# Biased attention with hash-routed experts: 640 slots per expert with an overflow branch, token ids carried in the rows, result rows scattered straight to the output

## The chip, the cores and the metric

The kernel runs on one core of one Trainium2 chip. The metric is device time in microseconds (us) of one execution. Times "of the trace" come from one profiled execution and count from the start of its span.

## The reference

What is computed, cut to what matters (`B=8, H=8, S=576, D=64`; `E=8` experts; `w1` is 512x1024 and `w2` 1024x512 for each expert, both float32):

```python
scores = scale * np.matmul(q, k.transpose(0, 1, 3, 2)) + bias      # bias by |i - j|, per head
attn = exp(scores - max) / sum
x = np.matmul(attn, v)  -> rows of 512 (B*S = 4608 tokens)
expert_idx = token_ids * 2654435761 % 8
for e in range(8):
    mask = expert_idx == e
    out[mask] = np.maximum(x[mask] @ w1[e], 0.0) @ w2[e]
```

With the token ids that are drawn, the experts get 584, 594, 556, 565, 570, 567, 568 and 604 tokens.

## The kernel before, in words

The kernel is written in a tile framework: the program gives loops and tiles, and a scheduler sets the order of each engine's instructions and all waits. An instruction that has nothing to wait for may be put well ahead of its place in the text; on its engine and queue the resulting order is then fixed, and a waiting instruction holds up what is behind it.

**Start.** SP's queue loads constants, the bias table and the token ids (`e2i`, L119: 4608 pieces of 4 bytes), then the first batch's `v` (L218, five loads of pieces of 256 bytes). TensorE and ScalarE make the exponentials of the bias (`ebsb`), which go to DRAM (`t5_ebp`, L111), are spread there to 128 shifted rows per head (`t5_ebr`, `load_ebias`, L195, one copy per head), and come back as one tile `ebias` per head (L203). VectorE meanwhile turns token ids into slots: 8 one-hot masks, prefix sums (L150 to L157) and a row offset from one small matmul; `ds2` holds, for each of 4608 tokens, expert * 768 + rank. One DMA on SP's queue (L357) fills the whole table `t5_xperm` (6144 rows of 512 float16, 6.29 MB) with zeros from a DRAM constant; it stands after batch 0 in the text, and the trace shows where it is issued.

**Attention.** For each of 8 batches, `q` and `k` are loaded on POOL's queue with a conversion from float32 to float16 (L224, L228; two batches of buffers), and for each of four head pairs `m`: transposes (L251), scores (L289), Exp on ScalarE out of PSUM (L297), multiplication by `ebias` on VectorE (L305), the product with `v` (L330), and division into `x_sb` (L348), which holds all tokens. At the end of a batch its 4 or 5 groups of 128 finished rows are scattered into `t5_xperm` by indirect DMAs on POOL's queue (L364). All of these write the same DRAM tensor, so each waits until the one before it has landed. In batch 4 the text has the load and cast of the first expert's `w1` (L373, L377).

**Experts.** For each expert: 768 rows of `t5_xperm` are loaded on SP's queue (`xpn`, L388) and transposed (24 transposes, L399, copied by VectorE, L404). The weights come as float32 on SP's queue (L414, L422; 2.10 MB each) and are cast by ScalarE (`w1`, L419) and VectorE (`w2`, L427). The first layer is 64 matmuls of 384 columns (L434), with a Relu on ScalarE for each four (L440); the second layer is 6 groups of 8 matmuls of 512 columns (L448), each copied by VectorE (`ok`, L455) and stored in slot order into the DRAM tensor `t5_pout` (L457).

**Tail.** When all of `t5_pout` is written, 36 indirect DMAs on POOL's queue gather 128 token rows each (`og`, L460), and SP's queue stores each to the output (L468).

Of the kernel before, what the change touches and what calls it, by code (L numbers as in the profile page):

```python
# [11 lines left out]
F32 = mybir.dt.float32  # L12
F16 = mybir.dt.float16
I32 = mybir.dt.int32
AF = mybir.ActivationFunctionType
# [16 lines left out]
def kernel(  # L32
# [23 lines left out]
    CAP = 768  # L56
    NSLOT = E * CAP
    NPT = DM // P
# [13 lines left out]
    SLT_np = np.triu(np.ones((P, P), dtype=np.float32), 1)  # L72
    Z_np = np.zeros((P, DM), dtype=np.float16)
# [4 lines left out]
    Z_d = nc.inline_tensor(Z_np, "t5_zero")  # L78
# [12 lines left out]
    w1f0 = cst.tile([P, NPT, F], F32, name="w1f0")  # L91
    w1h0 = cst.tile([P, NPT, F], F16, name="w1h0")

    with tc.tile_pool(name="su", bufs=1, side="right") as su, tc.tile_pool(
# [18 lines left out]
        sltsb = su.tile([P, P], F32, name="sltsb")  # L113
        nc.sync.dma_start(out=sltsb[:, :], in_=SLT_d.ap())

        tid32 = moe_token_ids.bitcast(I32)
# [6 lines left out]
        ei = su.tile([P, NGT], I32, name="ei")  # L123
        nc.vector.tensor_scalar(
            out=ei[:, :], in0=e2i[:, :], scalar1=E - 1, scalar2=None,
            op0=ALU.bitwise_and,
        )
        ef = su.tile([P, NGT], F32, name="ef")
        nc.vector.tensor_copy(out=ef[:, :], in_=ei[:, :])

        oh = su.tile([P, E, NGT], F32, name="oh")
        for e in range(E):
# [4 lines left out]
        rowtot = su.tile([P, E], F32, name="rowtot")  # L137
        nc.vector.tensor_reduce(
            out=rowtot[:, :], in_=oh[:, :, :], axis=mybir.AxisListType.X,
            op=ALU.add,  # L140
        )
        partA = sup.tile([P, E], F32, name="partA", space=bass.MemoryType.PSUM)
        nc.tensor.matmul(out=partA[:, :], lhsT=sltsb[:, :], rhs=rowtot[:, :])

        pa = su.tile([P, E, NGT], F32, name="pa")
        pb = su.tile([P, E, NGT], F32, name="pb")
        nc.vector.tensor_copy(out=pa[:, :, :], in_=oh[:, :, :])
        cur, nxt = pa, pb
        sh = 1
        while sh < NGT:  # L150
            nc.vector.tensor_copy(out=nxt[:, :, :sh], in_=cur[:, :, :sh])
            nc.vector.tensor_tensor(
                out=nxt[:, :, sh:], in0=cur[:, :, sh:],
                in1=cur[:, :, : NGT - sh], op=ALU.add,
            )
            cur, nxt = nxt, cur
            sh *= 2  # L157
        exc = nxt
        nc.vector.tensor_tensor(
            out=exc[:, :, :], in0=cur[:, :, :], in1=oh[:, :, :], op=ALU.subtract  # L160
        )
        for e in range(E):
            nc.vector.tensor_scalar(  # L163
                out=exc[:, e, :], in0=exc[:, e, :],
                scalar1=partA[:, e : e + 1], scalar2=None, op0=ALU.add,
            )
        nc.vector.tensor_tensor(
            out=exc[:, :, :], in0=exc[:, :, :], in1=oh[:, :, :], op=ALU.mult
        )
        rank = su.tile([P, NGT], F32, name="rank")  # L170
        nc.vector.tensor_reduce(
            out=rank[:, :], in_=exc[:, :, :].transpose([0, 2, 1]),
            axis=mybir.AxisListType.X, op=ALU.add,
        )
        dsf = su.tile([P, NGT], F32, name="dsf")
        nc.vector.tensor_scalar(
            out=dsf[:, :], in0=ef[:, :], scalar1=float(CAP), scalar2=None,
            op0=ALU.mult,
        )
        nc.vector.tensor_tensor(  # L180
# [318 lines left out]
```

## Time and profile before

| | us |
|---|---|
| median of three timed runs | 706.52 |
| lowest, highest | 705.2, 706.73 |
| span of the profiled execution | 705.6 |
| first multiplication by `ebias` (L305) | 57.4 |
| last division of the attention (L348) ends | 440.2 |
| first transpose of the experts (L399) | 461.5 |
| last matmul of the experts (L448) ends | 643.6 |

| engine | busy us | share of the span |
|---|---|---|
| PE (matmuls) | 556.6 | 79% |
| VectorE (DVE) | 343.5 | 49% |
| ScalarE (ACT) | 290.3 | 41% |
| GpSimd (POOL) | 139.7 | 20% |

How to read it: the span runs from the first to the last instruction of one execution, and the timed median is 0.9 us above it. The four marks of time cut it into a start (to 57), attention (to 440), a hand-over (to 461.5), the experts (to 643.6) and a tail. Shares of the whole span mix these stages, so each stage is read by itself.

### The profile page before, as it was taken

How to read it: one execution, taken by the hardware profiler on the slowest of the kernel's cores; microseconds unless marked ns; L12 is line 12 of the kernel's file. 1: busy time of each engine (PE TensorE's matmuls, PEld its weight loads, DVE VectorE, ACT ScalarE, POOL GpSimd, SP SyncE). 2: the span in 40 equal slices, each digit the busy share in tenths (PEclk: the TensorE clock that was granted, in tenths of full speed). 3: DMA queues.
4: the chain of work that ended last, by engine and by line, in shares of the span. 5: the costliest groups of instructions: out<-in, count | busy, mean ns of one | idle time of the engine just before them, and what ended most of it. 6: DMA issues, size and time to landing. Idle time of an engine off the chain costs nothing.

```text
span 705.6 us, 9655 instructions
## 1 busy us (share of the span) xinstructions
PE 556.6 (79%) x3656; PEld 287.1 (41%) x3656; DVE 343.5 (49%) x1150; ACT 290.3 (41%) x458; POOL 139.7 (20%) x156
## 2 busy tenths in 40 slices
PE   2626999999999999999999998089999999994000
PEld 0202545444444545454444544055555555552000
DVE  3305666666676766667666666024433343312000
ACT  1312365545545453645445463044466545440000
POOL 7213001412323124114110200200000000002772
PEclk9999999999999999999999999999999999998555
DMA  9999980900905819409300000197999997113998
GB/s 111 307 206 262 274 220 24 134 25 18 132 31 33 103 39 67 84 16 86 72 15 1 31 1 1 53 380 278 322 370 334 326 359 265 45 76 127 359 392 283
DMA packets 159614, 110.49 MB, mean 157 GB/s; under 512 B 120520, under 2 KB 131912, under 8 KB 159472
## 3 DMA queue, kind: packets, MB, share of 16 engines
q1 hardware_dynamic: 79952, 86.28, 39.0%
q0 software_dynamic: 79616, 23.60, 26.9%
q8 instruction: 28, 0.46, 0.3%
q14 instruction: 18, 0.15, 0.1%
HBM read 92.55 MB, written 35.54 MB: 182 GB/s over the span
## 4 chain that ended last, share of the span: by engine, by line
PE 64%; DMA 10%; ACT 9%; issue 5%; DVE 3%; POOL 3%; SPq 3%; POOLq 0%; ACTq 0%
PE px L330 22%; PE sc L289 15%; PE ops L448 11%; PE hps L434 11%; ACT attn L297 8%; DMA t_ebr<-t_ebp 3%; POOL og L460 3%; DVE attn L305 3%; PE psq L251 3%; SPq L218 2%; PE psk L251 2%; DMA t_xperm<-x_sb,ds 2%; DMA ebias<-t_ebr 1%; DMA w1f<-in_moe_w_dram 1%; PE xps L399 1%
## 5 line engine op out<-in xcount | busy, mean ns | idle before, releaser
L297 ACT ACTIVATE attn<-sc 128x576 f16<-128x576 f32 (+1 forms) x320 | 197.4, 647 | 224.6 <-PE sc L289 198.4
L330 PE MATMUL px<-vaug,attn 128*128 128x65 f16 (+3 forms) x1600 | 182.4, 243 | 20.0 <-DVE attn L305 16.8
L289 PE MATMUL sc<-qT,kT 64*128 64x512 f16 (+3 forms) x640 | 178.0, 428 | 24.6 <-ACT attn L297 24.4
L305 DVE TENSOR_TENSOR attn<-attn,ebias 128x576 f16<-128x576 f16 (+1 forms) x320 | 139.3, 452 | 90.5 <-ACT attn L297 57.6
L330 PEld LDWEIGHTS <-attn 128*128 128x128 f16 (+3 forms) x1600 | 117.4, 122 | 126.5 <-DVE attn L305 77.4
L440 ACT ACTIVATE h<-hps 128x384 f16<-128x384 f32 x128 | 62.2, 490 | 98.3 <-PE hps L434 97.5
L434 PE MATMUL hps<-xpt,w1h 128*128 128x384 f16 x512 | 86.6, 330 | 1.5 <-ACT h L440 1.5
L448 PE MATMUL ops<-w2h,h 128*128 128x512 f16 x384 | 86.6, 379 | 0.0
L364 POOL DMA_INDIRECT t_xperm<-x_sb,ds x36 | 37.6, 1044 | 243.6 <-DVE x_sb L348 178.2
L289 PEld LDWEIGHTS <-kT 64*128 64x128 f16 (+1 forms) x640 | 46.4, 116 | 79.6 <-issue 71.5
L460 POOL DMA_INDIRECT og<-t_pout,ds x36 | 34.1, 947 | 205.3 <-DMA t_pout<-ok 193.2
L348 DVE TENSOR_SCALAR x_sb<-px,rcp 128x64 f16<-128x64 f32 (+1 forms) x320 | 70.0, 274 | 1.6
L434 PEld LDWEIGHTS <-w1h 128*128 128x128 f16 x512 | 50.6, 99 | 36.3 <-issue 3.5
L455 DVE COPY ok<-ops 128x512 f32<-128x512 f32 x48 | 33.1, 691 | 59.5 <-PE ops L448 53.3
L448 PEld LDWEIGHTS <-h 128*128 128x128 f16 x384 | 37.1, 98 | 41.2
L224 POOL DMA_DIRECT2D qb<-in_q_dram x40 | 35.4, 886 | 82.7 <-PE psk L251 73.8
L404 DVE COPY xpt<-xps 128x768 f16<-128x768 f16 x32 | 17.2, 556 | 62.5 <-PE xps L399 61.6
L343 DVE RECIPROCAL rcp<-px 64x1 f32<-64x1 f32 (+1 forms) x128 | 18.7, 167 | 51.9 <-PE px L330 48.9
L251 PE MATMUL psq<-ident,qb 128*128 128x128 f16 (+1 forms) x160 | 35.6, 292 | 9.0 <-DVE pb L163 5.1
L228 POOL DMA_DIRECT2D kb<-in_k_dram x40 | 35.3, 882 | 21.9 <-DMA kb<-in_k_dram 21.8
L251 PE MATMUL psk<-ident,kb 128*128 128x128 f16 (+1 forms) x160 | 36.3, 297 | 0.0
L399 PE MATMUL xps<-ident,xpn 128*128 128x128 f16 x192 | 15.9, 230 | 22.1 <-DMA xpn<-t_xperm 22.1
(37 smaller groups left out, 182.5 us busy)
## 6 DMA issues: line engine op xcount, KB each, us to landing
w1f<-in_moe_w_dram SPq DMA_DIRECT2D x8, 2048.0 KB
w2f<-in_moe_w_dram SPq DMA_DIRECT2D x8, 2048.0 KB
t_pout<-ok SPq DMA_DIRECT2D x48, 256.0 KB
out_dram<-og SPq DMA_DIRECT2D x36, 256.0 KB
vb<-in_v_dram SPq DMA_DIRECT2D x32, 256.0 KB
xpn<-t_xperm SPq DMA_DIRECT2D x8, 768.0 KB
ebias<-t_ebr SPq DMA_DIRECT2D x8, 720.0 KB
qb<-in_q_dram POOLq DMA_DIRECT2D x32, 128.0 KB
```

The source lines that it names most:

```text
L224: nc.gpsimd.dma_start(out=qb16[:nt, t, :, :], in_=q[b, :, P * t : P * t + nt, :].transpose([1, 0, 2]),)
L251: nc.tensor.transpose(out=pst[:, P * t : P * t + nt], in_=srct[:nt, t, 2 * m : 2 * m + 2, :], identity=ident[:nt, :nt],)
L289: nc.tensor.matmul(out=scps[hh][:nt, ns:ne], lhsT=kT[64 * hh : 64 * hh + 64, P * t : P * t + nt], rhs=qT[64 * hh : 64 * hh + 64, ns:ne], s ...
L297: nc.scalar.activation(out=attn[hh][:nt, t, :], in_=scps[hh][:nt, :], func=AF.Exp, bias=0.0, scale=scale,)
L305: nc.vector.tensor_tensor(out=attn[hh][:nt, t, :], in0=attn[hh][:nt, t, :], in1=ebias[2 * m + hh][:nt, NJT - 1 - t, :], op=ALU.mult,)
L330: nc.tensor.matmul(out=px[nbase : nbase + isz, c, :], lhsT=attn[hh][:nt, t, i0c : i0c + isz], rhs=vaug[hh][:nt, t, :], start=(imm == 0), s ...
L348: nc.vector.tensor_scalar(out=x_sb[nbase : nbase + isz, gt, h * D : (h + 1) * D], in0=px[nbase : nbase + isz, c, :D], scalar1=rcp[nbase : ...
L364: nc.gpsimd.indirect_dma_start(out=xperm_d.ap()[:, :], out_offset=bass.IndirectOffsetOnAxis(ap=ds2[:, g : g + 1], axis=0), in_=x_sb[:, g, ...
L434: nc.tensor.matmul(out=hps[:, :], lhsT=w1h[:, kt, ts(ft, P)], rhs=xpt[kt][:, ts(nr, NR)], start=(kt == 0), stop=(kt == NPT - 1),)
L440: nc.scalar.activation(out=h1[:, ft, ds(nr * NR, NR)], in_=hps[:, :], func=AF.Relu, bias=0.0, scale=1.0,)
L448: nc.tensor.matmul(out=ops[:, :], lhsT=h1[:, ft, ts(kc, P)], rhs=w2h[:, ft, :], start=(ft == 0), stop=(ft == NFT - 1),)
L460: nc.gpsimd.indirect_dma_start(out=og[:, :], out_offset=None, in_=pout_d.ap()[:, :], in_offset=bass.IndirectOffsetOnAxis(ap=ds2[:, g : g + ...
```

## The change

The change touches everything but the middle of the attention.

- Each expert has 640 slots in place of 768, so its loops run over 5 blocks of rows in place of 6, and the first layer's matmuls have 320 columns in place of 384. The Relu is one instruction for 640 columns.
- A row of `t5_xperm` has 514 float16 (1028 bytes): 512 of `x` and the token's number as one int32. `t5_xperm` gets 4608 further rows, where tokens over an expert's 640 go. The fill writes only the 5120 slot rows (5.26 MB), with zeros and a number beyond the output, from an SBUF tile; it is issued on ScalarE's queue, and stands in batch 0's second head pair.
- The scatters into `t5_xperm` are declared disjoint and no longer wait for each other.
- The weights are loaded with conversion to float16 on POOL's queue, into two fixed buffers each for `w1` and `w2`; the casts on ScalarE and VectorE are gone. Experts 0 and 1 are loaded at places in the text after batches 3 and 5; the load for expert e+2 waits for expert e's last use of the buffer.
- `t5_pout`, the gathers and the tail's stores are gone: each 128 result rows go by one indirect DMA on POOL's queue to the output rows that their token numbers name; numbers beyond the output are skipped. These scatters are declared disjoint too.
- Token ids come as 36 contiguous rows and are transposed on TensorE; the prefix sums are one scan.
- At the end each engine reads a flag (an expert has more than 640 tokens) and branches: only with the flag set, a fallback of loops over all token groups and experts runs. With the counts above it isn't set.

The diff, cut (the arithmetic of the slots and the fallback's body are left out):

```diff
-    CAP = 768
+    CAP = 640
     NSLOT = E * CAP
+    NROW = NSLOT + B * S
+    BIG = 1 << 20
...
-    xperm_d = nc.dram_tensor("t5_xperm", [NSLOT, DM], F16, kind="Internal")
-    pout_d = nc.dram_tensor("t5_pout", [NSLOT, DM], F32, kind="Internal")
+    XW = DM + 2
+    xperm_d = nc.dram_tensor("t5_xperm", [NROW, XW], F16, kind="Internal")
...
+    w1t = [cst.tile([P, NPT, F], F16, name=f"w1t{i}") for i in range(2)]
+    w2t = [cst.tile([P, NFT, DM], F16, name=f"w2t{i}") for i in range(2)]
+
+    def disjoint(x, group):
+        i = getattr(x, "ins", x)
+        tc.declare_no_dep(
+            i, group=group,
+            reason="each token has a row of its own, so these writes are disjoint",
+        )
+        tc.add_to_no_dep_group(group, i)
+
+    def load_w1(e):
+        nc.gpsimd.dma_start(
+            out=w1t[e % 2][:, :, :],
+            in_=moe_w1[e].rearrange("(kt p) f -> p kt f", p=P),
+        )
+
+    def load_w2(e):
+        nc.gpsimd.dma_start(
+            out=w2t[e % 2][:, :, :],
+            in_=moe_w2[e].rearrange("(ft p) d -> p ft d", p=P),
+        )
...
-        e2i = su.tile([P, NGT], I32, name="e2i")
-        with nc.allow_non_contiguous_dma("tiny index reshape"):
-            nc.sync.dma_start(
-                out=e2i[:, :],
-                in_=bass.AP(tid32.tensor, 0, [[2, P], [2 * P, NGT]]),
-            )
+        er = su.tile([NGT, 2 * P], I32, name="er")
+        nc.sync.dma_start(
+            out=er[:, :],
+            in_=bass.AP(tid32.tensor, 0, [[2 * P, NGT], [1, 2 * P]]),
+        )
...
-        x_sb = at.tile([P, NGT, DM], F16, name="x_sb")
+        x_sb = at.tile([P, NGT, XW], F16, name="x_sb")
+        nc.vector.tensor_copy(
+            out=x_sb[:, :, DM:XW].bitcast(I32), in_=tok[:, :].unsqueeze(2)
+        )
...
+            if b == 0:
+                zx = at.tile([P, XW], F16, name="zx")
+                nc.vector.memset(zx[:, :DM], 0.0)
+                nc.vector.memset(zx[:, DM:XW].bitcast(I32), BIG)
...
+                if b == 0 and m == 1:
+                    nc.scalar.dma_start(
+                        out=xperm_d.ap()[:NSLOT, :].rearrange(
+                            "(p r) d -> p r d", p=P
+                        ),
+                        in_=zx[:, :].unsqueeze(1).to_broadcast(
+                            [P, NSLOT // P, XW]
+                        ),
+                    )
...
-            if b == 0:
-                nc.sync.dma_start(
-                    out=xperm_d.ap().rearrange("(a b) d -> a (b d)", b=64),
-                    in_=bass.AP(
-                        Z_d.ap().tensor, 0, [[0, NSLOT // 64], [1, 64 * DM]]
-                    ),
-                )
             for g in range((b * S) // P, ((b + 1) * S) // P):
-                nc.gpsimd.indirect_dma_start(
+                sc_in = nc.gpsimd.indirect_dma_start(
...
-            if b == 4:
-                nc.sync.dma_start(
-                    out=w1f0[:, :, :],
-                    in_=moe_w1[0].rearrange("(kt p) f -> p kt f", p=P),
-                )
-                nc.scalar.copy(out=w1h0[:, :, :], in_=w1f0[:, :, :])
+                disjoint(sc_in, "xrows")
+            if b == 3:
+                load_w1(0)
+                load_w2(0)
+            if b == 5:
+                load_w1(1)
+                load_w2(1)
...
+        xn = {0: x_load(0), 1: x_load(1)}
+        xt = {0: x_transpose(xn[0])}
         for e in range(E):
...
+            if e + 2 < E:
+                xn[e + 2] = x_load(e + 2)
+            w1h, w2h = w1t[e % 2], w2t[e % 2]
             h1 = mo.tile([P, NFT, CAP], F16, name="h1", bufs=2)
-            for nr in range(NRC):
-                for ft in range(NFT):
-                    hps = mop.tile([P, NR], F32, name="hps", bufs=3, space=bass.MemoryType.PSUM)
+            for ft in range(NFT):
+                hps = mop.tile([P, NRC, 512], F32, name="hps", bufs=2,
+                               space=bass.MemoryType.PSUM)
+                for nr in range(NRC):
                     for kt in range(NPT):
                         nc.tensor.matmul(
-                            out=hps[:, :],
+                            out=hps[:, nr, :NR],
...
+                nc.scalar.activation(
+                    out=h1[:, ft, :].rearrange("p (r n) -> p r n", r=NRC),
+                    in_=hps[:, :, :NR], func=AF.Relu, bias=0.0, scale=1.0,
+                )
+            if e + 2 < E:
+                load_w1(e + 2)
+            if e + 1 < E:
+                xt[e + 1] = x_transpose(xn[e + 1])
...
-                ok = mo.tile([P, DM], F32, name="ok", bufs=4)
+                ok = mo.tile([P, DM], F32, name="ok", bufs=8)
                 nc.vector.tensor_copy(out=ok[:, :], in_=ops[:, :])
-                kg = e * (CAP // P) + kc
-                nc.sync.dma_start(out=pout_d.ap()[ts(kg, P), :], in_=ok[:, :])
-        for g in range(NGT):
-            og = mo.tile([P, DM], F32, name="og", bufs=12)
-            nc.gpsimd.indirect_dma_start(
...
-            nc.sync.dma_start(out=out[ts(g, P), :], in_=og[:, :])
+                so = nc.gpsimd.indirect_dma_start(
+                    out=out[:, :],
+                    out_offset=bass.IndirectOffsetOnAxis(
+                        ap=xn[e][:, kc, DM:XW].bitcast(I32), axis=0
+                    ),
+                    in_=ok[:, :],
+                    in_offset=None,
+                    bounds_check=N - 1,
+                    oob_is_err=False,
+                )
+                disjoint(so, "orows")
+            if e + 2 < E:
+                load_w2(e + 2)
+
+    over = nc.values_load(flag[:1, :1], min_val=0, max_val=1)
+    with tc.If(over > 0):
...

```

## Rows read from the trace of the kernel before

**Rows 1.** Section 2 of the page, 40 equal slices: busy tenths of two engines

```profile
PE   2626999999999999999999998089999999994000
POOL 7213001412323124114110200200000000002772
```

**Rows 2.** Windows, experts: length, busy us (x instructions) by engine, clock, DMA share, GB/s

```profile
461.50:643.60 182.10, 180.52 (x1088) 100.03 (x1088) 67.19 (x87) 87.00 (x135) 0.00 (x0) 1.00 0.74 268
462.00:592.00 130.00, 128.46 (x799) 72.58 (x797) 51.10 (x65) 70.34 (x103) 0.00 (x0) 1.00 0.94 340
```

**Rows 3.** Chain that ended last, hand-over to the experts: start us, us, what

```profile
440.46 2.41 DMA t_xperm<-x_sb,ds
...
453.07 2.41 DMA t_xperm<-x_sb,ds
...
455.84 4.79 DMA xpn<-t_xperm
...
461.54 1.44 PE xps L399 x12
```

**Rows 4.** Chain that ended last, late experts and end of TensorE's work

```profile
578.56 10.40 PE hps L434 x64
...
600.70 10.40 PE hps L434 x64
...
633.24 10.37 PE ops L448 x48
...
643.64 0.70 DVE ok L455
...
644.36 1.99 DMA t_pout<-ok
```

**Rows 5.** Timeline of POOL in the tail: start, us, instruction, [idle before]

```profile
647.24 0.98 POOL L460 DMA_INDIRECT og<-t_pout,ds  x1 [193.21 <-DMA t_pout<-ok]
...
686.03 0.95 POOL L460 DMA_INDIRECT og<-t_pout,ds  x1 [0.30 <-issue]
688.34 0.94 POOL L460 DMA_INDIRECT og<-t_pout,ds  x1 [1.37 <-issue]
```

**Rows 6.** Chain that ended last, at the start

```profile
26.01 23.56 DMA t_ebr<-t_ebp
...
49.63 10.16 DMA ebias<-t_ebr
```

**Rows 7.** Timeline of SP's queue at the start

```profile
3.07 15.55 SPq L218 DMA_DIRECT2D vb<-in_v_dram  x5
...
19.84 0.56 SPq L357 DMA_DIRECT2D t_xperm<-t_zero  x1
...
80.05 16.01 SPq L218 DMA_DIRECT2D vb<-in_v_dram  x9
```

**Rows 8.** Timeline of SP's queue, last stores of the tail

```profile
695.10 7.04 SPq L468 DMA_DIRECT2D out_dram<-og  x11
```

**Rows 9.** Lines by form: busy, mean ns of one, idle before and releaser

```profile
L440 ACT ACTIVATE h<-hps 128x384 f16<-128x384 f32 x128 | 62.2, 490 | 98.3 <-PE hps L434 97.5
...
L404 DVE COPY xpt<-xps 128x768 f16<-128x768 f16 x32 | 17.2, 556 | 62.5 <-PE xps L399 61.6
...
L419 ACT CAST w1h<-w1f 128x4096 f16<-128x4096 f32 x7 | 25.2, 3603 | 13.2 <-DMA w1f<-in_moe_w_dram 13.1
```

**Rows 10.** Windows of the start, and of one batch's q and k loads

```profile
5.00:10.00 5.00, 3.58 (x6) 0.51 (x4) 0.00 (x0) 1.18 (x1) 5.00 (x8) 1.00 2.07 79
...
18.70:26.00 7.30, 2.45 (x20) 1.57 (x21) 3.52 (x16) 0.00 (x0) 3.81 (x5) 1.00 1.90 288
26.00:36.00 10.00, 9.38 (x45) 3.31 (x45) 2.17 (x10) 6.71 (x11) 0.00 (x0) 1.00 0.94 315
36.00:49.60 13.60, 3.05 (x13) 1.07 (x11) 0.00 (x0) 2.59 (x4) 0.88 (x1) 1.00 0.93 229
...
126.00:134.00 8.00, 8.00 (x45) 3.39 (x43) 4.92 (x16) 4.54 (x7) 6.96 (x9) 1.00 2.01 128
```

More of the change, by code (lines that the diff above doesn't have):

```diff
@@ L71 @@
     I128_np = np.eye(P, dtype=np.float16)
-    SLT_np = np.triu(np.ones((P, P), dtype=np.float32), 1)
-    Z_np = np.zeros((P, DM), dtype=np.float16)
+    SLT_np = np.triu(np.ones((P, P), dtype=np.float16), 1)
+    TOK_np = (np.arange(NGT)[None, :] * P + np.arange(P)[:, None]).astype(np.int32)
     OH_d = nc.inline_tensor(OH_np, "t5_bias_oh")
@@ L90 @@
     ds2 = cst.tile([P, NGT], I32, name="ds2")
-    w1f0 = cst.tile([P, NPT, F], F32, name="w1f0")
-    w1h0 = cst.tile([P, NPT, F], F16, name="w1h0")
+    tok = cst.tile([P, NGT], I32, name="tok")
+    nc.sync.dma_start(out=tok[:, :], in_=TOK_d.ap())
+    ef = cst.tile([P, NGT], F32, name="ef")
+    ovf = cst.tile([P, NGT], F32, name="ovf")
+    flag = cst.tile([1, 1], I32, name="flag")
+    w1t = [cst.tile([P, NPT, F], F16, name=f"w1t{i}") for i in range(2)]
[17 more added lines that the diff above has]
+        )
     with tc.tile_pool(name="su", bufs=1, side="right") as su, tc.tile_pool(
@@ L136 @@
             )
-        rowtot = su.tile([P, E], F32, name="rowtot")
+        rps = sup.tile([P, 2, 512], F32, name="rps", space=bass.MemoryType.PSUM)
+        EN = E * NGT
+        ohf = oh[:, :, :].rearrange("p e g -> p (e g)")
+        nc.tensor.matmul(out=rps[:, 0, :EN], lhsT=sltsb[:, :], rhs=ohf)
+        nc.tensor.matmul(out=rps[:, 1, :EN], lhsT=onesb[:, :], rhs=ohf)
+        inc = su.tile([P, E, NGT], F32, name="inc")
+        incf = inc[:, :, :].rearrange("p e g -> p (e g)")
+        nc.vector.tensor_tensor_scan(
+            out=incf, data0=keep[:, :, :].rearrange("p e g -> p (e g)"),
+            data1=rps[:, 1, :EN], initial=0.0, op0=ALU.mult, op1=ALU.add,
+        )
@@ L138 @@
+        mx = su.tile([P, 1], F32, name="mx")
         nc.vector.tensor_reduce(
-            out=rowtot[:, :], in_=oh[:, :, :], axis=mybir.AxisListType.X,
-            op=ALU.add,
-        )
[L142 to L154, printed above, removed]
-            )
-            cur, nxt = nxt, cur
-            sh *= 2
-        exc = nxt
+            out=mx[:, :], in_=inc[:, :, NGT - 1], axis=mybir.AxisListType.X,
+            op=ALU.max,
+        )
+        nc.vector.tensor_scalar(
+            out=flag[:, :], in0=mx[:1, :], scalar1=float(CAP), scalar2=None,
+            op0=ALU.is_gt,
+        )
@@ L159 @@
         nc.vector.tensor_tensor(
-            out=exc[:, :, :], in0=cur[:, :, :], in1=oh[:, :, :], op=ALU.subtract
+            out=incf, in0=incf, in1=rps[:, 1, :EN], op=ALU.subtract
         )
[L162 to L165, printed above, removed]
-            )
         nc.vector.tensor_tensor(
-            out=exc[:, :, :], in0=exc[:, :, :], in1=oh[:, :, :], op=ALU.mult
+            out=incf, in0=incf, in1=rps[:, 0, :EN], op=ALU.add
@@ L179 @@
+        sel = su.tile([P, NGT], F32, name="sel")
+        nc.vector.scalar_tensor_tensor(
+            out=sel[:, :], in0=ef[:, :], scalar=float(CAP), in1=rank[:, :],
+            op0=ALU.mult, op1=ALU.add,
+        )
+        dlt = su.tile([P, NGT], F32, name="dlt")
+        nc.vector.tensor_scalar(
+            out=dlt[:, :], in0=tok[:, :], scalar1=float(NSLOT), scalar2=None,
+            op0=ALU.add,
         )
         nc.vector.tensor_tensor(
-            out=dsf[:, :], in0=dsf[:, :], in1=rank[:, :], op=ALU.add
+            out=dlt[:, :], in0=dlt[:, :], in1=sel[:, :], op=ALU.subtract
@@ L182 @@
         )
-        nc.vector.tensor_copy(out=ds2[:, :], in_=dsf[:, :])
+        nc.vector.tensor_tensor(
+            out=dlt[:, :], in0=dlt[:, :], in1=ovf[:, :], op=ALU.mult
+        )
+        nc.vector.tensor_tensor(
+            out=ds2[:, :], in0=dlt[:, :], in1=sel[:, :], op=ALU.add
+        )
     with tc.tile_pool(name="at", bufs=1) as at, tc.tile_pool(
@@ L447 @@
+            for kc in range(NSC):
+                ops = mop.tile([P, DM], F32, name="ops", bufs=2,
+                               space=bass.MemoryType.PSUM)
                 for ft in range(NFT):
```

187 lines of the change are left out of this document (132 added, 55 removed).

## The prediction

> **What bounds the kernel now.** I read the slices of the page first [rows 1]: TensorE is close to full from a sixth of the span to nine tenths, with a hole in between and an empty stretch at the end, in which POOL alone works. So the kernel is one TensorE pipeline with three places where TensorE waits: the start, the hand-over from attention to experts, and the tail. The windows of the expert stage [rows 2] show TensorE busy for 180.52 of 182.10 us, while the DMA engines run at 0.94 of their time and 340 GB/s for most of it: bound by matmuls, with little DMA room. The chain of waits then gives each hole a cause. Hand-over: five scatters, one landing before the next is issued, then one load [rows 3]. Tail: the last matmul ends at 633.24 + 10.37 = 643.6 [rows 4], and then 36 gathers are issued 1.25 us apart [rows 5] and stored. Start: the chain is one DMA after another, of which a copy of `ebr` takes 23.56 us and the `ebias` after it 10.16 [rows 6]; SP's timeline shows why [rows 7]: the fill of 6.29 MB was issued at 19.84 on the same queue, ahead of it. I leave the 383 us of steady attention alone; no term below is in it.
>
> **The change, part by part**, against the profiled execution's 705.6 us.
>
> *Tail.* Now 705.6 - 643.6 = 62.0 us. Afterwards: the last copy `ok` 0.70 [rows 4], one scatter of 256 KB, and the end. The scatter of 128 KB took 2.41 from issue to landing [rows 3], the plain store of 256 KB 1.99 [rows 4]; I take 3.0. After the last landing the kernel needs 1.5 us to close: the last stores were issued by 695.10 + 7.04 = 702.1 [rows 8], 1.99 later they were in place, and the span ends at 705.6. The flag's load and the branch over the fallback have no row. Their lower bound is 0 (beside the scatter's landing); the nearest row is the one POOL instruction with a hole of 1.37 us instead of 0.30 before it [rows 5], and five engines with several such holes one behind the other make 7. I take 3. Sum 0.7 + 3.0 + 1.5 + 3 = 8.2, so **-54** (-47 to -57).
>
> *Hand-over.* Now 461.54 - 440.46 = 21.1. The five scatters no longer wait, so they follow each other as the gathers do, 0.95 + 0.30 = 1.25 apart [rows 5]: 4 x 1.25 + 2.41 = 7.4 in place of 15.0. Then 0.4 until SP issues the load, 4.79 for it [rows 3] (768 rows now, 640 then: 4.0 in proportion), and the 0.9 that follow. Sum 12.7 to 13.5, so **-8** (-5 to -9.5). Rows of 1028 bytes no longer start on even addresses, and the trace has no such rows: I add nothing, and up to 3 us in the range. The Trainium skill (DMA: Bandwidth & Descriptors, "How a descriptor splits into AXI transactions") speaks against the change here: transactions are 256 bytes and begin on multiples of 256, so a 1028-byte row takes five where a 1024-byte row took four. By that rule the load would be an estimated 5.0 us (4.0 x 5/4) and the hand-over's term about -7. No run so far shows it.
>
> *Experts.* One expert takes 600.70 - 578.56 = 22.14 us of TensorE [rows 4]: 10.40 for 64 matmuls of 384 columns (162.5 ns each), 10.37 for 48 of 512 (216 ns each), and 1.37 for 24 transposes. Afterwards 64 x 162.5 x 320/384 = 8.67, 40 x 216 = 8.64, 20/24 x 1.37 = 1.14: 18.45 us, and for eight 147.6. With 2.4 for the first transposes and the filling of the pipeline, 150 in place of 182.1: **-32**. What must hide: the Relu of 640 columns, at most 490 x 640/384 = 817 ns [rows 9], lies beside 8 matmuls of 1.08 us, with two buffers; VectorE's 4 copies of at most 556 ns and 5 of 0.70 are 5.7 us of 18.45. The casts (3.6 us each on ScalarE [rows 9]) were beside matmuls except at the first experts, so taking them away gives at most the 182.1 - 8 x 22.14 = 5.0 us by which the stage is longer than its steady pace, and that is in the -32.
>
> The weights for experts 2 to 7 must come through POOL's queue at that pace. In one period the DMA engines move 4.19 MB of weights (as read), 0.66 MB of `xpn` and about 1.18 MB of results: 6.0 MB in 18.45 us is 327 GB/s, against 340 in the window of now [rows 2]. So it just fits, counted by bytes read; counted by bytes written the weights are half. POOL's converting loads of `q` and `k` moved 128 GB/s of float16 [rows 10], that is 256 GB/s as read, in pieces of 256 bytes and paced by POOL's issues. At 256 a period would take 4.19/0.256 = 16.4 us for the weights and 5.6 for the rest at 327, 22.0 in place of 18.45. The load of each `w1` starts when its buffer's expert has done its first layer and is wanted about 1.5 periods (28 us) later, which covers a first delay of some 9 us but not six. Bounds: 0, and (22.0 - 18.45) x 6 - 9 = 12. Pieces of 2 and 4 KB are nearer to the loads of now than to those of 256 bytes: I take 0. POOL issues 7 DMAs in a period, about 1.25 us each, under 9 of 18.45; queued behind a waiting `load_w1` are only the scatters of the same expert, which nobody waits for until a buffer `ok` comes round, 8 groups later.
>
> *Start.* From 18.7 to 49.6 the chain waits for `ebp` and `ebr`, and the engines move 7.3 x 288 + 10 x 315 + 13.6 x 229 = 8.4 MB [rows 10], of which the fill is 6.29. Without it the other 2.1 MB would take 7.7 us at the same mean rate, 23 less. Further, five `v` loads kept SP until 18.6 (15.55 us), while nine later ones took 16.01, or 8.9 for five [rows 7]: the token ids in pieces of 4 bytes were in front of them. That is a gain of up to 6.7, so the far end is about -28. But the bytes remain: 5.26 MB of fill, now on ScalarE's queue. It waits for two memsets alone, as the zero fill waited for nothing, and that one was issued at 19.84 though it stands behind a whole batch in the text; so it can start in the first microseconds or beside `ebr`. And 8.4 MB of weights for experts 0 and 1 wait for nothing either; if they too are put into POOL's first idle time, about 25 us, they compete with `ebr` and `ebias` (8.4 MB / 340 GB/s = 25 us), and the start gains nothing or loses up to 6. On separate queues I take it that each gets about half: half of 23 is **-12** (-26 to +6). The Trainium skill (DMA: Bandwidth & Descriptors, "Queues, rings and completion order") says that each DMA engine goes round robin over the queues it has work for; by that rule `ebr` would share with the fill rather than stand behind it. In this trace fill and `ebr` lie on one queue, so it doesn't show it.
>
> The other edits (token number into `x_sb`, the scan, slots) are VectorE instructions of under 1 us each while VectorE waits for the start's DMAs.
>
> **Sum:** 705.6 - 54 - 8 - 32 - 12 = 599.6; the median stands 0.9 above the span, so 600.5. I give 600.
>
> **The rivals.**
> - *The weight stream paces the experts.* For it: 327 of 340 GB/s wanted. Against: the loads of now reach 340 beside stores. Price +12, with the unaligned rows up to +24: 612 to 624.
> - *The start gains nothing*, since fill and weights only change queue. For it: the bytes, and how far ahead the fill stood now. Price +12, up to +18: 612 to 618.
> - *The start gains most* because the fill really comes after the first heads' `ebias`: -14, so 586 and less.
> - *The scatters still wait* (the declaration doesn't take): hand-over +8, tail +3, in the experts 5 x 3.15 = 15.8 us of POOL's 18.45 and thus late weights: about 615.
> - *Slower than before: starved experts.* If the converting loads of large pieces run far below those of `q` and `k`, every period becomes the load's time. To lose 106 us in six periods each must be 18.45 + 17.7 = 36.1 us, which leaves 30.5 for 2.1 MB of float16: below 69 GB/s written it is slower than before. At 60 a period is 40.6 and the result 600 + 6 x 22.2 = 733. The lowest busy row, 79 GB/s from 5 to 10 us [rows 10], has the ids' 4-byte pieces in it; 128 speaks against.
>
> **How the numbers follow.** Forecast (588 to 611) 0.52; weight stream 0.18; start without gain 0.13; start with most 0.11; scatters that wait 0.03; starved 0.03. The range 580 to 628 leaves out the starved case, the far ends of the first two rivals together, and a start and tail that both come out at their best: under 2 in 10. A difference under 0.2% (1.4 us) is about what a measurement of this kernel can't tell from none; of the cases only a stream near 69 GB/s comes there. Faster 0.96, same 0.01, slower 0.03.
>
> **What would show it.** Tail: from the last matmul to the end of the span under 12 us, no DMA into `og`. Hand-over: five scatters 1.25 apart, first transpose 13 us after the first of them. Experts: 18.5 us from one expert's first matmul to the next's, PE without waits for the weight tiles. Start: first multiplication by `ebias` at about 45 and not 57; the fill's issue before or after `ebr`. The prediction is wrong if PE waits for `w1t` or `w2t` from expert 2 on, if the first multiplication stays at 57, or if the branch costs over 10 us.

## The result and the profile after

The median is 647.9 us (647.33 to 651.03) against 706.62 (705.2 to 707.12) for the kernel before: a ratio of 0.918, 95% interval 0.916 to 0.920. The forecast was 600.0, with a range of 580 to 628, so the time lies 48 us above the forecast and 20 above the upper end of the range. The profiled execution has a span of 645.5 us. The granted clock of TensorE is 1.00 (the level of 2.4 GHz) in the windows up to 620 us, and 0.50 (1.2 GHz) from 640 us on, when TensorE has nothing left to do.

Where the span went, stage by stage (us), with the marks of the prediction:

| stage | before | after | change | forecast |
|---|---|---|---|---|
| start and attention, to the first of the last five scatters | 440.5 | 471.9 | +31.4 | -12 |
| hand-over, to the first transpose | 21.1 | 13.2 | -7.9 | -8 |
| experts, to the last matmul | 182.1 | 150.0 | -32.1 | -32 |
| tail | 62.0 | 10.4 | -51.6 | -54 |
| sum | 705.6 | 645.5 | -60.1 | -106 |

Three terms of four came out within 2.4 us of the forecast. Of the miss of 46 us, 43 are in the first.

The chain that ended last, around the hand-over and for three of the eight experts (start us, us, what; of before: [rows 3, 4]):

```profile
475.69 0.96 POOL t_xperm L420
476.95 2.48 DMA t_xperm<-x_sb,ds
480.01 4.22 DMA xpn<-t_xperm
484.23 0.88 issue
485.10 0.70 PE xps L459 x5
...
506.90 8.69 PE hps L478 x64
...
525.38 8.69 PE hps L478 x64
...
543.85 8.69 PE hps L478 x64
...
626.45 8.65 PE ops L496 x40
635.12 0.70 DVE ok L503
```

The last scatter follows the one before it by 1.26 us and no longer waits for its landing; the load of rows of 1028 bytes takes 4.22. (Such rows begin on multiples of 4 bytes only; "uneven" stands for that from here on, and "even" for rows that begin on multiples of 128 bytes or more.) From expert to expert it is 525.38 - 506.90 = 18.48 us, with 18.45 forecast. Everything from 472 us on is as worked out.

The chain at the start of after is another matter (same columns; of before: [rows 6]):

```profile
1.64 44.27 DMA t_xperm<-zx
45.92 7.11 DMA vb<-in_v_dram
...
58.25 11.04 DMA t_ebp<-ebsb
...
69.92 8.13 DMA t_ebr<-t_ebp
...
78.07 14.78 DMA ebias<-t_ebr
```

The fill of the table is issued at 1.64 us and lands 44.27 later; behind it comes a load of `v`, and only then the store `t5_ebp` with which the bias path begins (before, its later link `ebr` was already under way at 26.01). The first multiplication by `ebias` stands at 87.28 us instead of 57.44, and 30 of the 31 us are lost there. VectorE's timelines of before (first row) and after (second), and POOL's first of the last five scatters in after (third), which ends the stage:

```profile
57.44 1.93 DVE L305 TENSOR_TENSOR attn<-attn,ebias 128x576 f16<-128x576 f16 x5 [23.50 <-DMA ebias<-t_ebr]
```

```profile
87.28 1.92 DVE L368 TENSOR_TENSOR attn<-attn,ebias 128x576 f16<-128x576 f16 x5 [23.34 <-DMA ebias<-t_ebr]
```

```profile
471.89 0.96 POOL L420 DMA_INDIRECT t_xperm<-x_sb,ds  x1 [43.45 <-DVE x_sb L411]
```

SP's and POOL's timelines and SP's waits say who is held up (start, us, instruction, [idle before]; the row of waits is engine, line, releaser: us in total, times, longest; of before: [rows 7]):

```profile
3.62 54.51 SPq L268 DMA_DIRECT2D vb<-in_v_dram  x10
58.25 0.73 SPq L138 DMA_DIRECT2D t_ebp<-ebsb  x1
```

The same loads in two shorter windows, the last six of them behind the landing of the fill:

```profile
7.24 16.55 SPq L268 DMA_DIRECT2D vb<-in_v_dram  x2
```

```profile
45.92 12.21 SPq L268 DMA_DIRECT2D vb<-in_v_dram  x6
```

POOL's timeline and SP's waits:

```profile
7.58 0.94 POOL L278 DMA_DIRECT2D kb<-in_k_dram  x1
11.78 0.69 POOL L274 DMA_DIRECT2D qb<-in_q_dram  x1 [3.26 <-DMA qb<-in_q_dram]
22.86 0.68 POOL L278 DMA_DIRECT2D kb<-in_k_dram  x1 [10.39 <-DMA kb<-in_k_dram]
30.23 0.88 POOL L274 DMA_DIRECT2D qb<-in_q_dram  x1 [6.69 <-DMA qb<-in_q_dram]
...
54.85 0.77 POOL L110 DMA_DIRECT2D w1t<-in_moe_w_dram  x1 [1.48 <-DMA qb<-in_q_dram]
```

```profile
SPq L268 <- DMA t_xperm<-zx: 22.1, 1, 22.1
```

Ten loads of `v`, those of batch 1 among them, stand ahead of `t5_ebp` on SP and keep it for 54.51 us. One of them waits 22.1 us for the fill itself, with which it shares no data. In the trace's records the DMAs that SP and ScalarE issue signal eight semaphores in turn, and each load of `v` from the second on waits for the DMA before it on its semaphore; the fill and this load have the same one. The loads of `q` and `k` on POOL's queue take turns over eight others in the same way, which is why each of them waits for an earlier one to land. Meanwhile POOL issues a load of `q` or `k` every 7 to 11 us where it takes 0.9 to issue one. The bytes that the engines move at that time are few (windows of after: length, busy us by engine, clock, DMA share, GB/s; before moved 288 and 315 GB/s from 18.7 to 36 [rows 10]):

```profile
20.00:30.00 10.00, 0.56 (x3) 0.22 (x3) 0.00 (x0) 0.00 (x0) 0.68 (x1) 1.00 1.34 180
30.00:40.00 10.00, 0.57 (x2) 0.20 (x2) 0.00 (x0) 0.00 (x0) 1.76 (x2) 1.00 1.35 167
```

And the queues from 20 to 45 us (packets, MB, time of their packets as a share of 16 engines; q10 carries the fill, q1 is SP's queue, q0 POOL's):

```profile
q10 hardware_dynamic: 2759, 2.82, 60.8%
q1 hardware_dynamic: 3129, 0.79, 40.7%
q0 software_dynamic: 3567, 0.45, 39.1%
```

The three queues are served about equally *in packets* (2759 to 3567), and so very unequally in bytes: 2.82 MB of fill against 0.45 of `q` and `k`.

### The profile page after: what moved, and what is told of

Same layout as the page of the kernel before. It is cut to its first block, busy times and chain, and to the rows that moved or that the text cites. A ratio compares the mean times of both kernels' runs of the same rounds, so it can differ in the third digit from the quotient of the medians.

```text
span 645.5 us, 9277 instructions
## 1 busy us (share of the span) xinstructions
PE 526.1 (82%) x3561; PEld 278.4 (43%) x3561; DVE 315.6 (49%) x1126; ACT 245.3 (38%) x386; POOL 159.3 (25%) x176
## 3 DMA queue, kind: packets, MB, share of 16 engines
q10 hardware_dynamic: 5136, 5.26, 4.3%
## 4 chain that ended last, share of the span: by engine, by line
PE 63%; DMA 14%; issue 9%; ACT 8%; DVE 3%; POOL 1%; POOLq 0%; SPq 0%
PE px L393 21%; PE sc L352 14%; PE hps L478 11%; PE ops L496 11%; ACT attn L360 8%; DMA t_xperm<-zx 7%; PE psq L314 3%; DVE attn L368 2%; DMA ebias<-t_ebr 2%; PE psk L314 2%; DMA t_ebp<-ebsb 2%; PE xps L459 2%; DMA t_ebr<-t_ebp 1%; DMA vb<-in_v_dram 1%; POOL t_xperm L420 1%
## 5 line engine op out<-in xcount | busy, mean ns | idle before, releaser
L393 PE MATMUL px<-vaug,attn 128*128 128x65 f16 (+3 forms) x1600 | 182.1, 243 | 24.7 <-DVE attn L368 22.0
L484 ACT ACTIVATE h<-hps 128x640 f16<-128x640 f32 x64 | 45.1, 704 | 115.4 <-PE hps L478 115.0
L496 PE MATMUL ops<-w2t,h 128*128 128x512 f16 x320 | 72.7, 379 | 0.0
L478 PE MATMUL hps<-xpt,w1t 128*128 128x320 f16 x512 | 71.9, 301 | 0.0
L478 PEld LDWEIGHTS <-w1t 128*128 128x128 f16 x512 | 50.4, 98 | 21.0 <-issue 0.2
L504 POOL DMA_INDIRECT out_dram<-ok,xpn x40 | 39.3, 981 | 56.5 <-DVE ok L503 54.4
L463 DVE COPY xpt<-xps 128x640 f16<-128x640 f16 x32 | 15.1, 489 | 73.6 <-PE xps L459 72.6
L503 DVE COPY ok<-ops 128x512 f32<-128x512 f32 x40 | 27.7, 692 | 47.0 <-PE ops L496 47.0
L496 PEld LDWEIGHTS <-h 128*128 128x128 f16 x320 | 30.7, 98 | 33.5
L406 DVE RECIPROCAL rcp<-px 64x1 f32<-64x1 f32 (+1 forms) x128 | 18.7, 166 | 50.6 <-PE px L393 47.8
L314 PEld LDWEIGHTS <-qb 128*128 128x128 f16 (+1 forms) x160 | 19.8, 131 | 43.0 <-issue 26.1
## 6 DMA issues: line engine op xcount, KB each, us to landing
t_xperm<-zx ACTq DMA_DIRECT2D x1, 5140.0 KB, 44.3
```

What stands on the lines that cost most here:

```text
L314: nc.tensor.transpose(out=pst[:, P * t : P * t + nt], in_=srct[:nt, t, 2 * m : 2 * m + 2, :], identity=ident[:nt, :nt],)
L393: nc.tensor.matmul(out=px[nbase : nbase + isz, c, :], lhsT=attn[hh][:nt, t, i0c : i0c + isz], rhs=vaug[hh][:nt, t, :], start=(imm == 0), s ...
L478: nc.tensor.matmul(out=hps[:, nr, :NR], lhsT=w1h[:, kt, ts(ft, P)], rhs=xt[e][:, kt, ts(nr, NR)], start=(kt == 0), stop=(kt == NPT - 1),)
L484: nc.scalar.activation(out=h1[:, ft, :].rearrange("p (r n) -> p r n", r=NRC), in_=hps[:, :, :NR], func=AF.Relu, bias=0.0, scale=1.0,)
L496: nc.tensor.matmul(out=ops[:, :], lhsT=h1[:, ft, ts(kc, P)], rhs=w2h[:, ft, :], start=(ft == 0), stop=(ft == NFT - 1),)
L504: so = nc.gpsimd.indirect_dma_start(out=out[:, :], out_offset=bass.IndirectOffsetOnAxis(ap=xn[e][:, kc, DM:XW].bitcast(I32), axis=0), in_= ...
```

## The experiments

My theory after the result: the early fill takes turns, packet by packet, with the small packets of `v`, `q` and `k`; SP's queue, and on it the bias path, waits until that is over. Each price below is a stage of a span, or a median; between the three sets of runs that were timed together, before came out at 705.5 (the first four kernels), 701.7 (the next four) and 701.3 us (the last three), so a difference of some us between sets says nothing unless ratio and median agree.

| kernel | median us | ratio to before, 95% | first multiplication at | start term |
|---|---|---|---|---|
| after | 647.9 | 0.918 (0.916 to 0.920) | 87.3 | +31.4 |
| fill late | 615.5 | 0.871 (0.869 to 0.874) | 35.7 | -0.7 |
| weights late | 637.8 | 0.904 (0.901 to 0.906) | 76.9 | +19.4 |
| both late | 598.9 | 0.848 (0.845 to 0.850) | 35.3 | -20.2 |
| fill early, pieces of 8 KB | 629.0 | 0.891 (0.889 to 0.893) | 61.4 | +11.6 |
| fill early, rows of 1152 bytes | 633.6 | 0.903 (0.900 to 0.905) | 66.2 | +17.4 |

(The start term is the first of the last five scatters in the kernel's own trace, less 440.5.)

**Fill late.** The fill's tile is first written from a result of head pair 2, so that the fill can't leave before it.

```diff
-                if b == 0 and m == 1:
+                if b == 0 and m == 3:
+                    nc.vector.tensor_scalar(
+                        out=zx[:, :D], in0=x_sb[:, 0, 4 * D : 5 * D],
+                        scalar1=0.0, scalar2=None, op0=ALU.mult,
+                    )
                     nc.scalar.dma_start(
```

> The changed kernel with the fill alone made later: its SBUF tile is written from results of head pair 2 of batch 0, so the fill can't be issued before them. Theory (the fill, issued at 1.64 us on its own queue, takes the DMA engines in turn with the first loads and holds up SP's fifth v load until it lands at 45.9): the first loads land by about 15 us, the first multiplication by ebias comes at 45 to 55 in place of 87, and the time falls by 30 to 40, to 608 to 618. Rival (the 8.4 MB of weights for experts 0 and 1, issued at 55 to 61 ahead of ebr and ebias, are the cause): they still stand in POOL's first idle time, the first multiplication stays past 75, and the time is 636 or more.

615.5 us, as the theory said: 32 us of the start are the fill's early issue. SP now comes to `t5_ebp` at 13.28 with five loads of `v` ahead of it, not ten, and the first multiplication is at 35.67. But 52 us of earlier start became only 32: the chain of this kernel has these links (start us, us, what), where weights and bias path meet.

```profile
33.45 18.88 DMA t_ebr<-t_ebp
...
58.53 10.84 DMA t_ebr<-t_ebp
...
70.92 19.18 DMA vb<-in_v_dram
```

**Weights late.** The first weight tiles are first written by VectorE from `x_sb` of the batch behind which their loads stand in the text; the fill stays early.

```diff
             if b == 3:
+                gd = (b * S) // P
+                for wt in (w1t[0], w2t[0]):
+                    nc.vector.tensor_copy(
+                        out=wt[:1, 0, :1], in_=x_sb[:1, gd, :1]
+                    )
                 load_w1(0)
                 load_w2(0)
...
```

> The changed kernel with the weight loads of experts 0 and 1 alone made later: each waits for a result of batch 3 or 5. Theory (fill): the fill still lands at about 45 us and the chain of ebp, ebr, ebias still starts at 58; what the weights added to that chain, up to 8 us, is all that is gained: 640 to 648. Rival (weights): ebp, ebr and ebias take what they took before without them, and the time falls by 20 or more, to 628 or less.

637.8 us, 10 less than after. The fill's landing is unmoved (44.61), and `ebp`, `ebr` and `ebias` take 6.71, 4.43 and 7.78 us in place of 11.04, 8.13 and 14.78. So the rival that gave the weights the larger part is out, and the theory's share for them (640 to 648) was a little low.

**Both late.**

Both edits above together.

> The changed kernel with both made later, the fill and the weight loads of experts 0 and 1. Theory (fill first, weights second): first multiplication by ebias at 35 to 45 us, 595 to 605, that is below the run with the fill alone made later by 5 to 15. If the weights cost nothing once the fill is away: the same as that run. If neither is the cause: near 648.

598.9 us. VectorE's timeline has the first multiplication at 35.29:

```profile
35.29 1.93 DVE L372 TENSOR_TENSOR attn<-attn,ebias 128x576 f16<-128x576 f16 x5 [2.66 <-DMA ebias<-t_ebr]
```

The start is 51.6 us shorter than in after, where the fill alone gave 32.1 and the weights alone 12.0. The weights cost more once the fill is out of their way (20.2 - 0.7 = 19.5 us of start). With both out of the first microseconds, the start is 20.2 us shorter than before.

**Fill early, but in larger pieces.** The same bytes at the same place, from a tile of eight rows: 640 packets of 8 KB in place of 5120 of 1 KB.

```diff
-                zx = at.tile([P, XW], F16, name="zx")
+                zx = at.tile([P, 8, XW], F16, name="zx")
...
-                            "(p r) d -> p r d", p=P
+                            "(p r j) d -> p r (j d)", p=P, j=8
...
```

> The changed kernel with the fill at the same place and of the same bytes, but from a tile with eight rows, so that it goes in pieces of 8224 bytes in place of 1028 (640 in place of 5120). If the engines take turns piece by piece between the queues, the fill with its large pieces gets most of them and lands at 15 to 20 us in place of 46, the first loads follow, and the first multiplication by ebias comes 20 to 28 us earlier: 620 to 628. If only the bytes count, the fill lands at about 45 as now and the time stays at 645 to 650.

629.0 us, 1 us above the range that turns by packet gave and 16 below the one that bytes alone gave. The queues of this kernel from 8 to 20 us (same columns as above) show the turns one for one:

```profile
q10 hardware_dynamic: 557, 4.58, 90.3%
q0 software_dynamic: 558, 0.07, 9.0%
q1 hardware_dynamic: 546, 0.14, 8.8%
```

In 12 us the fill gets 4.58 of 4.79 MB, and its queue sends its last packets between 21 and 22 us; the others lose fewer turns in all. The engines move 402 GB/s in this kernel from 10 to 15 us, and SP's ten loads of `v` take 33.68 us, 21 less than in after:

```profile
3.55 33.68 SPq L268 DMA_DIRECT2D vb<-in_v_dram  x10
```

No row of it shows SP waiting for the fill.

**Fill early, rows of 1152 bytes.** A row gets 576 float16, so that it starts on a multiple of 128 bytes; the fill and everything else carry 12% more bytes.

```diff
-    XW = DM + 2
+    XW = DM + 64
+    XT = DM + 2
...
```

> The changed kernel with rows of 1152 bytes in place of 1028, so that every row starts on a multiple of 128 bytes; the fill stays early and has as many pieces, 12 per cent more bytes. The mean time of a packet of the fill was 86 ns with 1028 bytes, and 50 ns in the kernel before with 1024-byte rows. If the uneven starts were its price: 55 to 60 ns, the fill lands at 30 to 36 in place of 46, and the time is 632 to 640. If the price came from what ran beside it: 85 to 95 ns and 647 to 654.

633.6 us, and the fill, issued at 3.70, lands after 33.0 us though it has more bytes. From section 3 of the pages, the fill's queue in after and here:

```profile
q10 hardware_dynamic: 5136, 5.26, 4.3%
```

```profile
q10 hardware_dynamic: 5136, 5.90, 2.6%
```

0.043 x 645.5 x 16 / 5136 = 86 ns for a packet of 1028 bytes, and 0.026 x 632.6 x 16 / 5136 = 51 ns for one of 1152. The landing agrees: 5136 / 16 = 321 packets on each engine, times 35 ns, are 11.2 us, and it fell by 44.3 - 33.0 = 11.3. From 12 to 34 us this kernel shows the turns one for one (same columns), and POOL's timeline how far apart the loads of `q` and `k` come:

```profile
q10 hardware_dynamic: 4120, 4.75, 59.8%
q0 software_dynamic: 4121, 0.52, 35.9%
q1 hardware_dynamic: 4121, 1.04, 35.9%
```

```profile
17.52 0.88 POOL L280 DMA_DIRECT2D kb<-in_k_dram  x1 [4.67 <-DMA kb<-in_k_dram]
23.07 0.87 POOL L276 DMA_DIRECT2D qb<-in_q_dram  x1 [4.67 <-DMA qb<-in_q_dram]
```

The price shows in the fill alone: the load of `xpn` takes 4.49 us here and 4.22 in after, the scatter 2.46 and 2.48. A row's start and its length changed together, so no run says which of the two costs.

**The kernel before, with an early fill.** The old zero fill from DRAM on SP's queue is replaced by one from SBUF on ScalarE's queue, with the old rows of 1024 bytes.

```diff
+            if b == 0:
+                zx = at.tile([P, DM], F16, name="zx")
+                nc.vector.memset(zx[:, :], 0.0)
...
+                if b == 0 and m == 1:
+                    nc.scalar.dma_start(
+                        out=xperm_d.ap().rearrange("(p r) d -> p r d", p=P),
+                        in_=zx[:, :].unsqueeze(1).to_broadcast(
+                            [P, NSLOT // P, DM]
+                        ),
+                    )
...
-                nc.sync.dma_start(
-                    out=xperm_d.ap().rearrange("(a b) d -> a (b d)", b=64),
...
```

> The kernel before with one part of the change alone: the fill (here 6144 rows of 1024 bytes, from an SBUF tile of zeros) goes on ScalarE's queue from the same place in the text, and is issued in the first 2 us. Theory: the first loads are held up as in the changed kernel, the fill lands at 45 to 55, the first multiplication by ebias moves from 57 to 85 or later, and the time rises by 25 to 35, to 730 to 740. Rival (the start's loss comes from the weights or from other edits of the change): the time stays within 8 of 706. A side reading: pieces of 1024 bytes on even addresses against 1028 on uneven ones, by the mean time of a packet on that queue (86 ns in the changed kernel); if the uneven addresses cost, it is below 75 ns here.

722.1 us, ratio 1.029 (1.027 to 1.032): 20.4 above before in the same set, more than the rival allowed and less than the theory expected. The start is 17.5 us longer than before, with the first multiplication at 76.09. The direction is the theory's, and this one part of the change is enough for it. These packets are even: 0.027 x 719.0 x 16 / 6160 = 50 ns each, and the fill lands after 28.9 us, at 30.1; that fits the smaller size. SP's timeline:

```profile
4.01 44.03 SPq L218 DMA_DIRECT2D vb<-in_v_dram  x10
48.09 1.19 SPq L376 DMA_DIRECT2D w1f<-in_moe_w_dram  x1
49.39 1.29 SPq L111 DMA_DIRECT2D t_ebp<-ebsb  x1
```

Ten loads of `v` stand ahead of `t5_ebp` here as well, without one that waits for the fill. But the turns hold SP only until the fill has landed: by then three loads are issued, and the other seven take from 30.29 to 48.04 without it. And the edit moved more than the fill: the first load of `w1` (2.10 MB), which SP issues at 96.10 in before, is ahead of the store too, and the store takes 12.53 us to land in place of 6.73. So the 17.5 us are the fill's early issue with what the scheduler moved along with it, and not the turns alone.

**The bias store on another queue.** In both-late (first text) and in after (second text) `t5_ebp` is stored from ScalarE's queue and not behind the `v` loads on SP's.

```diff
-        nc.sync.dma_start(out=ebp_d.ap()[:, :], in_=ebsb[:H, :])
+        nc.scalar.dma_start(out=ebp_d.ap()[:, :], in_=ebsb[:H, :])
```

> The run with both made later, and besides ebp is stored from ScalarE's queue, right behind the exponentials, in place of SP's queue behind five v loads. If what now bounds the start is the chain ebp, ebr, ebias, ebr is issued 2 to 5 us earlier and the time is 594 to 597; if the first loads bound it, 597 to 600.

> The changed kernel with ebp alone moved to ScalarE's queue; the fill stays early and the weights too. Rival theory (the order on SP's queue, ten v loads ahead of ebp, is the cause, and not the fill): ebp leaves at 12 in place of 58, and the time falls by 15 or more. Theory (the fill holds up SP's queue and the loads): ebr still stands behind the v loads that wait for the fill, and the time falls by at most the 11 us that ebp took from issue to landing: 636 to 648.

Neither is faster: 599.0 us (ratio 0.853, 0.851 to 0.855) where both-late had 598.9 (0.848), and 647.1 (0.922, 0.920 to 0.924) where after had 647.9 (0.918). The first falls into the case that the first loads bound the start, the second into the theory's range. In the second the store left at 41.56 instead of 58.25, still behind the fill on its own queue, and `ebr`, which stayed on SP behind the ten loads, couldn't begin before 58.38. So this run doesn't isolate what the order on SP costs by itself, and that stays open.

**All of it.** Both late, `t5_ebp` on ScalarE's queue and pieces of 8 KB, by the edits above.

> As the run with both made later and ebp on ScalarE's queue, and besides the fill goes in pieces of 8224 bytes. The late fill of small pieces ran beside the v loads of the next batches for 36 us; with large pieces it should land in 12 to 18, and the second batch's first scores should come 0 to 6 us earlier: 588 to 597. If the late fill held up nothing, the same as the run without the large pieces.

598.2 us (597.36 to 598.91): the late fill lands after 15.7 us instead of 36.4 in both-late, and no instruction of either kernel is shown waiting for it. No gain over both-late, so the late fill held up nothing.

**Without the branch.** The flag's load, the branch and the fallback are left out.

```diff
-    over = nc.values_load(flag[:1, :1], min_val=0, max_val=1)
-    with tc.If(over > 0):
...
```

> The changed kernel without the flag's load, the branch and the fallback (left out: the fallback for experts with more than 640 tokens, which these counts never reach). The prediction's tail allowed 3 us for the branch; the trace has 9.4 us from the start of the last scatter to the end of the span. If the branch is on that path: 643 to 645, and about 6 from the last scatter to the end. If it lies beside the scatter's landing: no change, 647 to 649.

643.9 us (ratio 0.917, 0.915 to 0.920), within the expectation but not to be told from after by its ratio, since its first multiplication comes 1.9 us later (at 89.18). The end of the trace tells it: the last scatter is issued at 637.74 and the span ends at 643.7, 6.0 us later; in after it is 636.09 to 645.5, 9.4. The branch is on the path with 3.4 us.

**Scatters that wait.** Both declarations are left out, so each scatter waits for the landing of the one before it, in the attention and in the experts.

```diff
-                disjoint(sc_in, "xrows")
...
-                disjoint(so, "orows")
```

> The changed kernel without the two declarations that the scatters are disjoint, so that each waits for the one before it again. By the prediction's terms: hand-over 21 in place of 13 us, the experts' pace unchanged at 18.5 us if five waiting scatters (3.2 us each, 16 us) still fit beside it, the tail up to 3 longer: 656 to 660. If the waits on POOL's queue also make the weight loads late, the experts' pace rises to 19.5 or more and the time to 664 or more.

718.8 us (ratio 1.025, 1.020 to 1.029): 71 us more than after, and slower than before. That is in the second case's "664 or more", but 55 above its lower end, and not by late weights. The start is the same (first multiplication at 87.78). Hand-over 21.6 us in place of 13.2, experts 194.1 in place of 150.0, tail 29.4 in place of 10.4: +8.4, +44.1 and +19.0. POOL's timeline in the experts and TensorE's (start, us, instruction, [idle before <- releaser]), and the waits of the whole run:

```profile
562.15 1.00 POOL L503 DMA_INDIRECT out_dram<-ok,xpn  x1 [1.45 <-DMA out_dram<-ok,xpn]
570.63 0.97 POOL L503 DMA_INDIRECT out_dram<-ok,xpn  x1 [7.48 <-DMA out_dram<-ok,xpn]
```

```profile
570.87 1.25 PE L458 MATMUL xps<-ident,xpn 128*128 128x128 f16 x10 [8.39 <-DMA xpn<-t_xperm]
...
582.11 3.15 PE L477 MATMUL hps<-xpt,w1t 128*128 128x320 f16 x22
```

```profile
POOL out_dram L503 <- DMA out_dram<-ok,xpn: 105.9, 23, 7.7
```

A scatter issued behind a weight load on POOL's queue lands some 8 us later (562.15 to 570.63) instead of 2.5; the next scatter waits for that, the buffer `xpn`, from which the scatters read their row numbers, comes free late, and the next load of `xpn` with it. TensorE waits for rows, not for weights.

## Why the prediction failed, point by point

*Tail*: right. -51.6 for -54 (within -47 to -57). The branch, priced at 3 from one hole in POOL's timeline, is 3.4.

*Hand-over*: right, -7.9, and adding nothing for the uneven rows was right for the load. The Trainium skill's rule (DMA: Bandwidth & Descriptors, "How a descriptor splits into AXI transactions"), from which the prediction estimated 5.0 us, isn't seen in the load: 4.22, where bytes in proportion gave 4.0.

*Experts*: right, 150.0. The weights keep pace; the mean over the stage is 172 GB/s as written and a DMA share of 0.78, with TensorE busy for 149.90 us. The rival "the weight stream paces the experts" is out. The Relu of 640 columns takes 704 ns (bound 817), hidden as said.

*Start*: wrong in sign, +31.4 for -12, outside its own range of -26 to +6. Three steps of it failed.

1. "On separate queues I take it that each gets about half." Half of the bytes was meant. The queues share by packets. A packet of `q` or `k` pays a turn each time, that is one packet of the fill and one of `v` as well: a load of `q` or `k` in the row-1152 kernel comes every 5.56 us, which for 128 KB in packets of 126 bytes (0.52 MB in 4121), 64 on each engine, is 87 ns a turn, and 22 us for 4120 turns on 16 engines are 85. The Trainium skill's rule that the prediction cited (DMA: Bandwidth & Descriptors, "Queues, rings and completion order") says round robin *by packet*. The trace agrees as far as the profile's packets go, 4120 / 4121 / 4121; the page's packet has typically 9 to 17 descriptors, and how many one of the profile's has isn't shown. Carried through, rows of 1 KB against pieces of 256 bytes, the rule would have put the collision with the first loads into the term. In before with the early fill, whose rows are even, the start loses 17.5 us.
2. The prediction looked for the victim in `ebr`, as before. In after the fill is over when `ebr` starts; the victims are `v` on SP and `q` and `k` on POOL, and `t5_ebp` waits for its place on SP. The prediction had `v` only as a gain, up to 6.7 us from the token ids; it went from 15.55 us for five to 54.51 for ten. That an earlier fill lets more of `v` stand ahead of `t5_ebp` (ten and not five) is a scheduler's choice that the trace of before couldn't show.
3. A packet of 1028 bytes was costed by its bytes. As a write it takes 86 ns, where one of 1152 takes 51. The prediction put the uneven rows on the load, and nothing on the fill, which has eight times as many rows as one load of 640.

It said that the fill "can start in the first microseconds" and that weights in POOL's first idle time would compete with the bias path; both happened. Its "loses up to 6" was for the start as a whole, with about 25 us of weights against a gain of 23; the start loses 31.4, of which the weights are 12.0 (19.5 when the fill is late). So the weights cost less than the prediction allowed at worst, and the price that was missing is the fill's. One sum of the term is off too: its far end, 23 and 6.7, is -29.7 and not "about -28", and the range's -26 follows from neither; the miss lies on the other side. The step from "it may start early" to a gain was the error: I averaged a gain (the fill leaves `ebr`'s queue) with a collision that I had not priced by rows.

The rivals: "the start gains nothing" was the nearest, and its mechanism (fill and weights "only change queue") points the right way, but its price of +12 to +18 on the forecast should have been +43. The case in which the start gains most is what both-late shows: -20.2. Its 598.9 us lie 1 us from the forecast, but by another sum: a start 8 us shorter than forecast, and 176.7 us from the first of the last scatters to the end where 171.3 were forecast. So they don't confirm the term. "The scatters still wait, about 615" was mispriced by far: 718.8. It counted POOL's time per scatter (3.15 us), and not that a landing behind a weight load of 1 MB takes 8.

What stays open: how much of the 31 us is the wait of one `v` load for the fill's semaphore, how much the ten loads ahead of `t5_ebp` and how much the turns, since no run takes away one alone. The rows give the split of SP's 54.51 us in after: 20.2 for four loads beside the fill (3.62 to 23.80), 22.1 of waiting, and 12.2 for six loads after its landing. The five loads of batch 1, which in both-late stand behind the store, take 11.4 of that (46.69 to 58.13), and 12.3 each in the 8 KB kernel (24.92 to 37.23) and in before with the early fill (35.73 to 48.04), in all three with the fill gone. So an estimate from these rows is that some 12 us of the store's delay come from its place in the order. The even-rows kernel has 10.3 us of the wait, the 8 KB kernel none and 33.68 us of `v` loads nevertheless.

## What to carry to other kernels

A bulk transfer without inputs that was moved to its own queue started at once (1.64 us), and then took turns with everything else packet by packet: work out how many packets the small loads that the first compute waits for have to send, and what a turn costs with the bulk's packets between them; half of the bandwidth is not the answer. Give such a transfer something to wait for that comes after the first loads (32 us of start here), or send it in large pieces (20 us); and look at what the scheduler then puts ahead of the store that the first compute hangs on. Before pricing "the waits stay", look at which long transfers stand on the same queue between two waiters.

## What the runs showed of the hardware

Writes from SBUF to DRAM in rows of 1028 bytes took 86 ns a packet (78 to 93 in the kernels that issue the fill, or the weights, later); rows of 1024 bytes 50, of 1152 bytes 51, and pieces of 8224 bytes 306 (0.020 x 626.8 x 16 / 656), or 38 ns per KB. The rule of transactions of 256 bytes doesn't explain it: by it both a row of 1028 and one of 1152 bytes, starting on a multiple of 128, need five, and 1024 four (the Trainium skill, DMA: Bandwidth & Descriptors, "How a descriptor splits into AXI transactions"); the traces give 86, 51 and 50. Neither the load of 640 such rows nor the scatter of 128 showed the price. A store of 19 KB (`t5_ebp`) took between 5.59 and 12.78 us in these kernels, by what else was under way.
